# Mamba-2 scan and gated feed-forward: a 64-column scan state, multiplied with C in four 32-row products

## The chip, the cores and the metric

The kernel runs on one core of a Trainium2 chip. The time is that of one execution on the device, in microseconds (us); the kernel before took 407.95 us, the median of nine runs that lay between 407.56 and 408.33 us. The engines are called by the profile's names: PE multiplies matrices (PEld is its weight load), DVE, ACT and POOL work element by element, SP issues the DMAs.

## What is computed

Four sequences of 768 steps pass through a scan with 8 heads, of 32 channels and 16 state entries each. In the reference the scan goes in chunks; the kernel's own chunks are 128 steps long. Everything is 32-bit floating point.

```
for each chunk:
    cum   = cumsum(log a)
    M     = (C @ B^T) * exp(cum_i - cum_j) * causal
    y     = M @ x  +  (C @ state) * exp(cum)
    state = exp(sum log a) * state  +  sum_j B_j x_j exp(cum_last - cum_j)
tokens = y of the 8 heads side by side          # 3072 x 256
h      = tokens @ w_in                          # 3072 x 2048
out    = (h * cos(h)) @ w_out                   # 3072 x 256
```

The term that matters here is C @ state: for each head a 16 x 32 state is multiplied with the 16 rows of C of that head.

## The kernel before, in words

The work is cut in 6 chunks `c` of 128 steps. The four sequences `b` of a chunk make 512 tokens, and for each chunk the feed-forward goes through 16 slices `f` of 128 hidden columns. The main loop runs over n = (c, f), 96 steps and two more to finish. A step issues `first(n)` (h: two products of 128x128 weights with 512 tokens, tile hp, L373), `gate(n)` (cosine and product, DVE and ACT), and `second(n-2)` (four products with the 256 columns of w_out, tile o, L401). Between these, in the same step, one piece of the next chunk's scan is issued: `turn`, `intra` and `finish` of one sequence take three steps in turn (f = 3 to 14). So the order of PE's instructions is written out by hand, and the schedule is manual: every engine runs its own in that order.

For one sequence of a chunk, all 8 heads of 16 state entries lie in the 128 partitions, head h in rows 16h to 16h+15.

- `turn` transposes B and C (L290, L291). `bcT[:, 0]` is B, `bcT[:, 1]` is C times the decay (L299). `cT` holds two copies of C: `slot` is a column pair of ones and zeros that keeps in copy t the rows of heads whose number within its pair is t (L295).
- `intra` multiplies B and C of heads in four products (L309). Each uses 32 rows, that is one pair of heads, and writes 256 columns to a bank of its own. DVE multiplies the result with the decays (m, L313, two halves of four heads).
- `finish` makes y, transposed, in PSUM: 256 rows (8 heads of 32 channels) by 128 steps, as two blocks t of 128 rows (heads 0 to 3 and 4 to 7). First comes C @ state (L327): the state tile is 128 rows by 256 columns with zeros wherever row and column are of different heads, so that two products of 128 rows, 128 columns of weights and 128 moving columns give all heads at once. Then eight products (L331), one for each head, with 32 columns of weights, add M @ x. ACT copies y out (L336).
- At the end of `finish`, in chunks 1 to 4, `sum_up` makes B^T x in PSUM (s_ps, L348): four products, one for each pair of heads, 32 rows by 64 columns, of which the two blocks off the diagonal are of no use. `carry` (DVE) spreads s_ps over the 256 columns and masks it with `own` (L358), and adds the state before times its decay (L362). For chunk 0, `sum_up` and `carry` are issued in the loop's steps 1 and 2.

`own` is made at the start, on DVE and POOL (L218 to L221); `slot` is a sum of its columns (L225, L227). PSUM for the scan is a rotation of two pairs of banks (`pair`, tag "scan"): tp, two times g, y and s_ps take the pairs in turn, so that a tile waits until the one before the last was read.

In chunk 0 `finish` has no state term; it is given a bank by a tag, and fills with products that nobody reads (L94). From n = 0 to 13 the weights of the feed-forward, which arrive as 64-bit words, are also converted (`grade`, `join`: ACT, POOL, DVE).

Of the kernel before, what the change touches and what calls it, by code (L numbers as in the profile page):

```python
# [8 lines left out]
FP32 = mybir.dt.float32  # L9
# [3 lines left out]
ALU = mybir.AluOpType  # L13
# [12 lines left out]
def kernel(  # L26
# [23 lines left out]
    V, ACT, G, PE = nc.vector, nc.scalar, nc.gpsimd, nc.tensor  # L50

    NB, H, S, D = x.shape
    N = B.shape[-1]
    P = 128
# [5 lines left out]
    HH = H // 2  # L60
# [3 lines left out]
    HP = H // 2  # L64

    const = ctx.enter_context(tc.tile_pool(name="const", bufs=1))
    loads = ctx.enter_context(tc.tile_pool(name="loads", bufs=3))
    rows = ctx.enter_context(tc.tile_pool(name="rows", bufs=NB))
    scan = ctx.enter_context(tc.tile_pool(name="scan", bufs=2))
    states = ctx.enter_context(tc.tile_pool(name="states", bufs=NB + 1))  # L70
# [8 lines left out]
    def bank(shape, name, tag):  # L79
        return psum.tile(shape, FP32, tag=tag, bufs=2, name=name)  # L80

    def pair(name):

        return psum.tile([P, 2, 4 * P], FP32, tag="scan", bufs=2, name=name)
# [6 lines left out]
    def fill(dst, times=1):  # L91

        for _ in range(times):
            PE.matmul(dst, lhsT=ones, rhs=ones.unsqueeze(1).to_broadcast([P, dst.shape[1], P]),  # L94
                      start=True, stop=True, skip_group_check=True)
# [27 lines left out]
    def load_along(c, seqs=range(NB)):  # L123
# [15 lines left out]
        out=a_in, in_=a.rearrange("(u b) h (c p) -> (b h c) u p", u=NU, p=P))  # L139
# [65 lines left out]
    for n in (0, 2, 1, 3, 4, 5):  # L205
# [8 lines left out]
    unit = const.tile([P, HH, P], FP32, name="unit")  # L214
    V.tensor_copy(out=unit, in_=ident.unsqueeze(1).to_broadcast([P, HH, P]))

    own = const.tile([P, H, D], FP32, name="own")
    V.memset(own, 1.0)  # L218
    G.affine_select(out=own, in_=own, pattern=[[-N, H], [0, D]], compare_op=ALU.is_ge,
                    fill=0.0, base=0, channel_multiplier=1)  # L220
    G.affine_select(out=own, in_=own, pattern=[[N, H], [0, D]], compare_op=ALU.is_ge,  # L221
                    fill=0.0, base=N - 1, channel_multiplier=-1)

    slot4 = const.tile([P, HH], FP32, name="slot4")
    V.tensor_tensor(out=slot4, in0=own[:, 0:HH, 0], in1=own[:, HH:H, 0], op=ALU.add)  # L225
    slot = const.tile([P, 2], FP32, name="slot")
    V.tensor_tensor(out=slot, in0=slot4[:, 0:2], in1=slot4[:, 2:4], op=ALU.add)  # L227

# [14 lines left out]
    scaled, lam, reach, state, part, yT = {}, {}, {}, {}, {}, {}  # L243
# [73 lines left out]

    def finish(c, b, tag=None, fills=0):
        (bcT, m), xr = part.pop((c, b)), raw[c][1]
        y = (pair("y")[:, 0] if tag is None else bank([P, 4 * P], "y", tag)  # L320
             ).rearrange("p (k i) -> p k i", k=4)
        fill(y[:, 2:4], fills)
        y = y[:, 0:2]
        if c > 0:
            s = state[c - 1, b].rearrange("p h d -> p (h d)")
            for t in range(2):
                PE.matmul(y[:, t], lhsT=s[:, t * P:(t + 1) * P], rhs=bcT[:, 1],  # L327
                          start=(t == 0), stop=False, skip_group_check=True)
        for h in range(H):
            q, t = h % 4, h // 4  # L330
            PE.matmul(y[32 * q:32 * q + 32, t], lhsT=xr[:, b, h], rhs=m[:, h],  # L331
                      start=(c == 0 and t == 0), stop=True, tile_position=(0, 32 * q),
                      skip_group_check=True)
        if b == 0:
            yT[c] = two.tile([P, 2, TB], FP32, tag="yT", name="yT")
        ACT.copy(out=yT[c][:, :, b * P:(b + 1) * P], in_=y)  # L336
        if 0 < c < NC - 1:
            sum_up(c, b, pair("s_ps")[:, 0, 0:2 * D])
            carry(c, b)

    sums = {}

    def sum_up(c, b, s_ps):

        xr, sc = raw[c][1], scaled.pop((c, b))
        for q in range(4):
            two_ = slice(2 * q, 2 * q + 2)
            PE.matmul(s_ps[32 * q:32 * q + 32], lhsT=sc[:, two_].rearrange("p h n -> p (h n)"),  # L348
                      rhs=xr[:, b, two_].rearrange("p h d -> p (h d)"), start=True, stop=True,
                      tile_position=(0, 32 * q), skip_group_check=True)  # L350
        sums[c, b] = s_ps

    def carry(c, b):

        s_ps = sums.pop((c, b))
        state[c, b] = new = states.tile([P, H, D], FP32, tag="state", name="state")
        by_two = "p (k t) d -> p k (t d)"
        V.tensor_tensor(out=new.rearrange(by_two, k=HP),  # L358
                        in0=s_ps.unsqueeze(1).to_broadcast([P, HP, 2 * D]),
                        in1=own.rearrange(by_two, k=HP), op=ALU.mult)  # L360
        if c > 0:
            V.scalar_tensor_tensor(out=new, in0=state.pop((c - 1, b)),  # L362
                                   scalar=reach[c, b][:, P - 1:P], in1=new,
                                   op0=ALU.mult, op1=ALU.add)


    hp, turns, gT, o, o_full = {}, {}, {}, {}, {}
# [59 lines left out]
    decays(0, 2, 1)  # L427
    turn(0, 1)
    finish(0, 0, "o")
    intra(0, 1)  # L430
    grade(*order[0])
    spread_a(3, ("o", "h"))
    decays(0, 3, 0)
    decays(0, 3, 1)
    turn(0, 2, "h")
    finish(0, 1, "o", 1)
    intra(0, 2)
    turn(0, 3, "h")
    grade(*order[2])
    join(*order[0])  # L440
    finish(0, 2, "o", 1)
    intra(0, 3)
    grade(*order[1])
# [14 lines left out]
    for n in range(NC * NF + LAG):  # L458
        c, f = divmod(n, NF)
        rest = None  # L460
        if n < NC * NF:
            if f == 0 and c > 0:
                load(c + 2)
            first(n)
            if n == 1:
                for b in range(0, NB, 2):
                    s_ps = pair("s_ps")
                    for t in range(2):
                        sum_up(0, b + t, s_ps[:, t, 0:2 * D])
            if n + 3 < len(order):  # L470
                rest = grade(*order[n + 3], later=True)
            if n + 2 < len(order):
                join(*order[n + 2])
            for b in ((0, 1), (2, 3))[n - 1] if 0 < n < 3 else ():
                carry(0, b)
            gate(n)
            if rest:
                rest()
        if n >= LAG:
            second(n - LAG)  # L480
        if c + 1 < NC:
            b, j = divmod(f - 3, 3)
# [4 lines left out]
            b, j = divmod(f - 2, 3)  # L487
# [37 lines left out]
```

## Time and profile before

| | |
|---|---|
| median of nine runs | 407.95 us (407.56 to 408.33) |
| the profiled execution | 407.94 us, of which its span of instructions is 406.2 us |
| PE busy | 399.3 us, 2086 matmul instructions |
| DVE busy | 266.4 us, 412 instructions |
| ACT busy | 173.4 us |
| POOL busy | 43.6 us |
| granted clock of PE | 0.999 |

A 32-bit product appears in the trace as two matmul instructions and two weight loads, so L327 has 80 of them for 20 calls of `finish` with two products each. A row of a timeline gives the start, the time to the end of its last instruction, engine, line, operation, tiles and shapes, and the number of instructions that were merged. Matmuls overlap in the pipeline: their durations are longer than the time each one adds, and the distance from one start to the next is what counts. Of a wait, the profile names the engine and line that released it.

### The profile page before, as it was taken

Reading aid. Unit: us, or ns where it says so; the run is one execution under the profiler, and the core shown is the slowest. Engines: PE = TensorE matmul, PEld = TensorE weight load, DVE = VectorE, ACT = ScalarE, POOL = GpSimd, SP = SyncE. Lnnn points to the kernel's source line nnn. Section 1 sums busy time; section 2 is a strip of 40 time slices with the busy share of each in tenths; the row PEclk is TensorE's granted clock in tenths of the full one; section 3 lists DMA queues with packets and bytes.
Section 4 is the critical chain, followed back from the end, with each engine's and each line's share of the span. In section 5 each row is a group of like instructions: output and inputs, shape, how many; then the busy total and the mean of one; then the engine's idle time right before and its main releaser. Section 6 shows DMA issues by size and latency. Waiting matters only on the chain.

```text
span 406.2 us, 5538 instructions
## 1 busy us (share of the span) xinstructions
PE 399.3 (98%) x2086; PEld 261.7 (64%) x2086; DVE 266.4 (66%) x412; ACT 173.4 (43%) x329; POOL 43.6 (11%) x62
## 2 busy tenths in 40 slices
PE   8999999999999999999999999999999999999996
PEld 5646666666666666667666666666666566666664
DVE  6989999946767755677664677674576764433342
ACT  2576666434343424434334433433434343433332
POOL 2266555300000000000000000000000000000000
PEclk9999999999999999999999999999999999999999
DMA  7989899491111092110174211120100000100001
GB/s 112 270 255 223 232 261 181 124 112 53 52 52 53 13 158 64 53 51 3 52 122 61 71 34 52 53 78 1 54 0 2 0 0 2 52 0 2 0 1 52
DMA packets 106650, 30.53 MB, mean 75 GB/s; under 512 B 75328, under 2 KB 102528, under 8 KB 106624
## 3 DMA queue, kind: packets, MB, share of 16 engines
q1 hardware_dynamic: 106096, 29.92, 32.1%
q8 instruction: 16, 0.26, 0.3%
q10 hardware_dynamic: 528, 0.26, 0.2%
q14 instruction: 10, 0.08, 0.1%
HBM read 26.84 MB, written 3.34 MB: 74 GB/s over the span
## 4 chain that ended last, share of the span: by engine, by line
PE 94%; SPq 2%; DMA 1%; ACT 1%; DVE 1%; issue 0%; DVEq 0%
PE hp L373 42%; PE o L401 41%; PE g L309 4%; PE y L331 3%; PE y L327 2%; SPq L112 2%; DMA words<-in_moe_w_in_dram 1%; PE tp L290 1%; PE tp L291 1%; PE s_ps L348 0%; PE y L94 0%; ACT w L384 0%; DVE m L313 0%; DVE gT L386 0%; DVE w L379 0%
## 5 line engine op out<-in xcount | busy, mean ns | idle before, releaser
L373 PE MATMUL hp<-yT,w_in 128*128 128x512 f32 x384 | 184.8, 604 | 0.7 <-DVE gT L386 0.7
L401 PEld LDWEIGHTS o<-w_out,gT 128*128 128x128 f32 x768 | 145.9, 190 | 59.9 <-issue 44.0
L401 PE MATMUL o<-w_out,gT 128*128 128x256 f32 x768 | 181.1, 379 | 0.0
L377 ACT ACTIVATE k<-hp 128x512 int32<-128x512 f32 x96 | 57.3, 597 | 125.5 <-PE hp L373 125.4
L386 DVE TENSOR_TENSOR gT<-hp,w 128x512 f32<-128x512 f32 x96 | 66.3, 690 | 65.4 <-ACT w L384 65.4
L379 DVE SCALAR_TENSOR_TENSOR w<-hp,k 128x512 f32<-128x512 f32 x96 | 66.0, 687 | 62.4 <-ACT k L377 61.1
L373 PEld LDWEIGHTS hp<-yT,w_in 128*128 128x128 f32 x384 | 67.8, 190 | 58.4 <-issue 54.2
L384 ACT ACTIVATE w<-w,quarter 128x512 f32<-128x512 f32 x96 | 69.3, 722 | 77.8 <-DVE w L379 77.8
L274 DVE TENSOR_TENSOR_SCAN lam<-arow,unit 128x512 f32<-128x512 f32 x40 | 48.5, 1212 | 0.0
L313 DVE TENSOR_TENSOR m<-g,lam 128x512 f32<-128x512 f32 x48 | 30.7, 681 | 1.1 <-PE g L309 0.9
L283 POOL TENSOR_TENSOR sc<-bc,lam 128x128 f32<-128x128 f32 x20 | 8.2, 412 | 199.6 <-DVE lam L274 194.7
L295 ACT ACTIVATE cT<-tp,slot 128x128 f32<-128x128 f32 x48 | 14.6, 353 | 9.5 <-PE tp L291 9.5
L309 PE MATMUL g<-cT,bcT 32*128 32x256 f32 x192 | 17.2, 426 | 1.4 <-ACT bcT L297 1.4
L331 PE MATMUL y<-m,xr 128*32 128x128 f32 x384 | 15.8, 279 | 0.2 <-DVE m L313 0.2
L175 POOL TENSOR_SCALAR mag<-mag 128x512 f32<-128x512 f32 x16 | 13.0, 812 | 9.4 <-ACT mag L174 9.3
L195 DVE SCALAR_TENSOR_TENSOR mag<-words,mag 128x512 uint32<-128x512 uint32 x16 | 13.5, 841 | 0.6
L336 ACT COPY yT<-y 128x256 f32<-128x256 f32 x24 | 8.9, 372 | 11.0 <-PE y L331 11.0
L309 PEld LDWEIGHTS g<-cT,bcT 32*128 32x128 f32 x192 | 7.5, 182 | 9.0 <-issue 6.2
L327 PEld LDWEIGHTS y<-bcT,state 128*128 128x128 f32 x80 | 12.0, 191 | 1.4 <-DVE m L313 0.4
L327 PE MATMUL y<-bcT,state 128*128 128x128 f32 x80 | 12.3, 276 | 0.0
L174 ACT ACTIVATE mag<-words 128x512 f32<-128x512 f32 x16 | 10.8, 678 | 2.0 <-DMA words<-in_moe_w_in_dram 2.0
L331 PEld LDWEIGHTS y<-m,xr 128*32 128x32 f32 x384 | 8.9, 109 | 4.3 <-DVE m L313 1.4
(48 smaller groups left out, 152.1 us busy)
## 6 DMA issues: line engine op xcount, KB each, us to landing
arow<-a_cut SPq DMA_DIRECT2D x20, 512.0 KB
words<-in_moe_w_in_dram SPq DMA_DIRECT2D x8, 512.0 KB
words<-in_moe_w_out_dram SPq DMA_DIRECT2D x8, 512.0 KB
out_dram<-ob SPq DMA_DIRECT2D x10, 256.0 KB
xr<-in_x_dram SPq DMA_DIRECT2D x4, 512.0 KB
along<-a_all SPq DMA_DIRECT2D x20, 64.0 KB
xr<-in_x_dram SPq DMA_DIRECT2D x8, 128.0 KB
bc<-in_B_dram SPq DMA_DIRECT2D x4, 256.0 KB
```

The costliest lines, as they stand in the source:

```text
L274: V.tensor_tensor_scan(out=lam[c, b][:, hs].rearrange("p h i -> p (h i)"), data0=rows_.rearrange("p h i -> p (h i)"), data1=unit.rearrange ...
L295: ACT.activation(cT[:, t], tp[:, 1], AF.Copy, scale=slot[:, t:t + 1])
L309: PE.matmul(g[u // 2][:, u % 2, 0:2 * P], lhsT=bcT[r, 0], rhs=cT[r].rearrange("p t i -> p (t i)"), start=True, stop=True)
L313: V.tensor_tensor(out=m[:, hs].rearrange("p (k t) i -> p k (t i)", k=2), in0=g[u][:, :, 0:2 * P], in1=l[:, hs].rearrange("p (k t) i -> p k ...
L327: PE.matmul(y[:, t], lhsT=s[:, t * P:(t + 1) * P], rhs=bcT[:, 1], start=(t == 0), stop=False, skip_group_check=True)
L331: PE.matmul(y[32 * q:32 * q + 32, t], lhsT=xr[:, b, h], rhs=m[:, h], start=(c == 0 and t == 0), stop=True, tile_position=(0, 32 * q), skip ...
L373: PE.matmul(hp[n], lhsT=w_in[:, k, f * P:(f + 1) * P], rhs=yT[c][:, k], start=(k == 0), stop=(k == KT - 1))
L377: ACT.activation(k, hp[n], AF.Copy, bias=0.25, scale=INV_2PI)
L379: V.scalar_tensor_tensor(out=w, in0=hp[n], scalar=INV_2PI, in1=k, op0=ALU.mult, op1=ALU.subtract)
L384: ACT.activation(cos, cos, AF.Sin, bias=quarter, scale=TWO_PI)
L386: V.tensor_tensor(out=gT[n], in0=hp.pop(n), in1=cos, op=ALU.mult)
L401: PE.matmul(o[c][b], lhsT=g[:, b * P:(b + 1) * P], rhs=w_out[:, f], start=(f == 0 and (last or b % 2 == 0)), stop=(f == NF - 1), skip_grou ...
```

## The change

The state tile keeps, for each row, only the 64 columns of its own pair of heads (two blocks of 32), and the block of the other head is zero. The product with C becomes four: 32 rows (one pair of heads) by 64 columns of weights, each with a tile position of its own in PE's array. Products 0 and 1 write rows 0 to 63 and 64 to 127 of one bank, products 2 and 3 the same rows of a second bank. For chunk 0 the code keeps its one bank.

`carry` works on 64 columns: for chunk 0 one DVE instruction (s_ps times `slot`), later one DVE instruction (state times decay plus s_ps, to a new tile `whole`) and one POOL instruction that masks it with `slot`. `own` shrinks from 256 columns to 8.

```diff
-    own = const.tile([P, H, D], FP32, name="own")
+    own = const.tile([P, H], FP32, name="own")
     V.memset(own, 1.0)
-    G.affine_select(out=own, in_=own, pattern=[[-N, H], [0, D]], compare_op=ALU.is_ge,
+    G.affine_select(out=own, in_=own, pattern=[[-N, H]], compare_op=ALU.is_ge,
                     fill=0.0, base=0, channel_multiplier=1)
-    G.affine_select(out=own, in_=own, pattern=[[N, H], [0, D]], compare_op=ALU.is_ge,
+    G.affine_select(out=own, in_=own, pattern=[[N, H]], compare_op=ALU.is_ge,
                     fill=0.0, base=N - 1, channel_multiplier=-1)
...
-    V.tensor_tensor(out=slot4, in0=own[:, 0:HH, 0], in1=own[:, HH:H, 0], op=ALU.add)
+    V.tensor_tensor(out=slot4, in0=own[:, 0:HH], in1=own[:, HH:H], op=ALU.add)
...
     def finish(c, b, tag=None, fills=0):
         (bcT, m), xr = part.pop((c, b)), raw[c][1]
-        y = (pair("y")[:, 0] if tag is None else bank([P, 4 * P], "y", tag)
-             ).rearrange("p (k i) -> p k i", k=4)
-        fill(y[:, 2:4], fills)
-        y = y[:, 0:2]
         if c > 0:
-            s = state[c - 1, b].rearrange("p h d -> p (h d)")
-            for t in range(2):
-                PE.matmul(y[:, t], lhsT=s[:, t * P:(t + 1) * P], rhs=bcT[:, 1],
-                          start=(t == 0), stop=False, skip_group_check=True)
+
+            y = pair("y")[:, :, 0:P]
+            for q in range(4):
+                r, p = slice(32 * q, 32 * q + 32), 64 * (q % 2)
+                PE.matmul(y[p:p + 64, q // 2], lhsT=state[c - 1, b][r].rearrange("p t d -> p (t d)"),
+                          rhs=bcT[r, 1], start=True, stop=False, tile_position=(32 * q, p),
+                          skip_group_check=True)
+        else:
+            y = bank([P, 4, P], "y", tag)
+            fill(y[:, 2:4], fills)
+            y = y[:, 0:2]
...
     def carry(c, b):
-        s_ps = sums.pop((c, b))
-        state[c, b] = new = states.tile([P, H, D], FP32, tag="state", name="state")
-        by_two = "p (k t) d -> p k (t d)"
-        V.tensor_tensor(out=new.rearrange(by_two, k=HP),
-                        in0=s_ps.unsqueeze(1).to_broadcast([P, HP, 2 * D]),
-                        in1=own.rearrange(by_two, k=HP), op=ALU.mult)
-        if c > 0:
-            V.scalar_tensor_tensor(out=new, in0=state.pop((c - 1, b)),
-                                   scalar=reach[c, b][:, P - 1:P], in1=new,
-                                   op0=ALU.mult, op1=ALU.add)
+
+        s_ps = sums.pop((c, b)).rearrange("p (t d) -> p t d", t=2)
+        mask = slot.unsqueeze(2).to_broadcast([P, 2, D])
+        state[c, b] = new = states.tile([P, 2, D], FP32, tag="state", name="state")
+        if c == 0:
+            V.tensor_tensor(out=new, in0=s_ps, in1=mask, op=ALU.mult)
+            return
+        whole = scan.tile([P, 2, D], FP32, tag="whole", name="whole")
+        V.scalar_tensor_tensor(out=whole, in0=state.pop((c - 1, b)),
+                               scalar=reach[c, b][:, P - 1:P], in1=s_ps,
+                               op0=ALU.mult, op1=ALU.add)
+        G.tensor_tensor(out=new, in0=whole, in1=mask, op=ALU.mult)
```

## The prediction

> **What bounds the kernel now.** I read the busy times first, then the chain of work that ended last, then PE's waits, and then the timeline of PE around `finish`.
>
> ```profile
> PE 399.3 (98%) x2086; PEld 261.7 (64%) x2086; DVE 266.4 (66%) x412; ACT 173.4 (43%) x329; POOL 43.6 (11%) x62
> ...
> PE 94%; SPq 2%; DMA 1%; ACT 1%; DVE 1%; issue 0%; DVEq 0%
> PE hp L373 42%; PE o L401 41%; PE g L309 4%; PE y L331 3%; PE y L327 2%; SPq L112 2%; DMA words<-in_moe_w_in_dram 1%; PE tp L290 1%; PE tp L291 1%; PE s_ps L348 0%; PE y L94 0%; ACT w L384 0%; DVE m L313 0%; DVE gT L386 0%; DVE w L379 0%
> ```
>
> PE is busy nearly all of the span and is 94% of the chain. A busy PE could still be a PE that is held up, so its waits come next.
>
> ```profile
> PE g L309 <- ACT bcT L297: 1.4, 3, 0.9
> PE warm L94 <- DVE quarter L212: 1.1, 1, 1.1
> PE hp L373 <- DVE gT L386: 0.7, 1, 0.7
> PE y L331 <- DVE m L313: 0.2, 1, 0.2
> ```
>
> That is all, 3.4 us, and all of it before 28 us. Since matmuls are pipelined, a short hold can hide in a busy PE; the distances between starts show two more, named below, of 0.04 and 0.14 us. Otherwise what an instruction adds is the distance from its start to the next. So the time moves with what PE's queue holds, and with nothing else unless something new comes late.
>
> **The place of the change on PE.** This is one `finish` (chunk 1, sequence 1); the other 19 have the same steps to within a few ns, but for the very first.
>
> ```profile
> 55.38 0.38 PE L401 MATMUL o<-w_out,gT 128*128 128x256 f32 x1
> 55.59 0.61 PE L327 MATMUL y<-bcT,state 128*128 128x128 f32 x4
> 56.13 0.64 PE L331 MATMUL y<-m,xr 128*32 128x128 f32 x16
> 56.59 0.29 PE L348 MATMUL s_ps<-xr,sc 128*32 128x64 f32 x8
> 56.81 1.13 PE L373 MATMUL hp<-yT,w_in 128*128 128x512 f32 x2
> ```
>
> From the last o to the first y of L331 it is 0.75 us; single starts, to the ns, make it 216 + 537. The 216 is the ordinary step of an o product (256 columns). The 537 is four instructions (two products, two each) at 109 ns, and then 101 ns before L331 begins: the last L327 instruction is followed by L331 after 205 ns, not 109, because L331 takes 32 columns of the array at a time and the ones before took all of it. I call this a **switch**; L331's first weights, too, are loaded only then.
>
> What four 32-row products cost is shown by g (L309), which has four of them with 256 moving columns:
>
> ```profile
> 63.81 0.38 PE L401 MATMUL o<-w_out,gT 128*128 128x256 f32 x1
> 64.12 0.71 PE L309 MATMUL g<-cT,bcT 32*128 32x256 f32 x8
> 64.76 1.13 PE L373 MATMUL hp<-yT,w_in 128*128 128x512 f32 x2
> ...
> 64.44 0.39 PE L309 MATMUL g<-cT,bcT 32*128 32x256 f32 x4
> ```
>
> The last line is the second half of the same eight (from a later window). The eight start as two groups of four, and within a group 7 ns apart: the four products run side by side. From the last o to the first group it is 309 ns, that is 216 plus a switch of about 94; to the second group 320, that is 216 plus 104 of weight load that nothing hides; from there to hp 324, that is 216, 20 of stagger and a switch of 88.
>
> **Part 1, the product with C.** The instruction orders of the two programs differ here by just this: at each of 20 places two L327 products become four, of 64 columns of weights and 128 moving columns. If they run side by side like g's, the steps are:
> - last o to the first group: 309, as for g.
> - first to second group: 109 for 128 columns, and the exposed load. It is 104 for 128 columns of weights (g) and 25 for 32 (L331: first group to second 134 where the next ones are 109). Between these lie 64 columns; I take half of 104, 52. Together 161.
> - second group to L331: 109, stagger 20, switch 90: 219. L331's own first load is in both kernels.
>
> Sum 689 ns against 753: 64 ns less, 19 times, 1.22 us. The first `finish` is different: its L327 starts 355 after the o before, as it waits for a bank that DVE reads until 42.71 us (m), and it takes 641. There the switch costs nothing, since PE waits anyway: 355 + 161 + 219 = 735 against 996. The second half of m ends at 43.31, and L331's second four heads would come at 43.39, so up to 20 ns of the 261 go; 0.24 us. Together **1.46 us**.
>
> The bounds of this part. A switch from one partition of the array to another isn't in the trace: L331 to s_ps (both 32 columns wide) costs none, every other one 88 to 95. If it is free, 20 x 90 = 1.8 us more are gained. If both groups' loads are exposed, at 52 to 104, 20 x (52 to 104) = 1.0 to 2.1 us are given back.
>
> **Part 2, carry.** L358 (424 ns, 20 times) and L362 (485, up to 673 beside POOL, 16 times) become one DVE instruction of 64 columns from PSUM. L299, which reads 128 columns of PSUM, takes 292; a line through it and L358 gives 226 for 64. For bounds, at least 165 (the smallest DVE rows with two inputs are 168) and at most L362's 485. DVE is relieved of about 11.5 us, beside PE, which waits for DVE nowhere after chunk 0 but in two places: the first `finish` above, whose m hangs on ACT's bcT (DVE idles 0.36 us before L299 at 38.1 us) and so doesn't come sooner; and an hp at 31.1 us, where the step from o is 259 instead of 216 because the gT before it (L386) stands behind two carries. That one loses its 43 ns: **0.04 us**.
>
> **Part 3, the mask on POOL.** 16 new instructions of 64 columns; L283, 128 columns, is 412 ns, so between 206 and 412; I take 250. What is behind it in POOL's queue: in chunk 1 (four times) mag (L175) and the join of weights (L199); later only sc. Mag waits for ACT, idle 1.11 and 1.26 us before two of them, as the next step's k and Abs come first, while the mask is ready some 0.6 us after s_ps. So it is covered; without cover it would be 4 x 0.4 = 1.6 us at most, and only if weights become late, which hp shows nowhere now. The state itself is read only a chunk later: the one written at 58 us at 120. POOL also slows DVE when they run together (L362 is 483 alone and up to 673 beside POOL); in chunk 1 m is still 0.26 us ahead of L331 at the second `finish`, and later over 2 us. Nothing on the path.
>
> **Part 4, the start.** `own` shrinks: L219 and L221 (450 and 444 ns on POOL) become two of at least 104 (POOL's smallest row), and cut comes about 0.6 us sooner. The chain at the start doesn't pass there: SP issues loads until 10.74, the weights' first words land at 15.09 and ACT goes on from them. Nothing gained. If that cover weren't there, 0.6 us.
>
> Sum: 1.46 + 0.04 = 1.5 us of the profiled 407.94, which is 0.01 below the median. That gives **406.4 us** (span 404.7).
>
> **A rule that speaks against it.** Products 0 and 1 take different rows of the array and write the same bank, in different partitions. No row of this trace has that: g's four have a bank each, and L331's four share a bank but take all rows. The Trainium skill, TensorEngine Tiling (Array Packing), Gotcha 1: PSUM Pressure, says that different row tiles can't access one PSUM bank at the same time. By that rule the four would go at best two at a time, and the time would be that of the first rival. I go with the rows, as each of the two ways of sharing runs four wide by itself.
>
> **Rivals.**
> 1. *Products that share a bank take turns* (slower). For it: no row shows two row tiles in one bank. Against: L331's four column tiles share one and start 7 ns apart. Two at a time means four groups instead of two: 2 x 109 x 20 = 4.4 us on top of the forecast, 410.8. The point from which it decides is one group more: 109 - 64 = 45 ns a `finish`, 0.9 us, 408.8. With none side by side, eight groups, 6 x 109 x 20 = 13.1 us on top, 419.5.
> 2. *The switch between two tiled partitions is free* (faster). For it: L331 to s_ps. Against: that is the same partition. 406.4 - 1.8 = 404.6.
> 3. *The gain is eaten by exposed loads and switches* (no change): four narrow products side by side, but both loads exposed. For it: g's first load. Against: g's second is hidden behind 216 ns; here there are 109 to hide 52. 407.4 to 408.5.
>
> **How the numbers follow.** Forecast 0.62, with a range of its own of 405.4 to 407.1 (half a switch either way); rival 2 0.08; rival 3 0.11; rival 1 0.19, of which 410.8 is the likeliest. Leaving out rival 1 leaves 0.81, so the range runs from rival 2 to the upper end of rival 3, to just below its one extra group: 404.4 to 408.7. About 0.2%, 0.8 us, is what a measurement of this kernel tells from no change: below 407.1 are the forecast and rival 2, 0.70; within it rival 3, 0.11; above, rival 1, 0.19.
>
> **What would show it.** In the profile after: the state products as two groups of four, 7 ns apart, 0.16 us between; L331 0.38 us after their first start and 0.69 after the last o. Four groups: rival 1. A distance from the last group to L331 of 0.13 instead of 0.22: rival 2. DVE busy about 11 us lower, with PE waits unchanged. I am wrong if PE waits anew, for m, the mask or weights, or if the groups are more than two.

## The result and the profile after

The changed kernel takes 406.77 us, the median of nine runs (406.51 to 407.06); before, with more runs, it is 408.17. The ratio is 0.9964, its 95% interval 0.9955 to 0.9973: 1.5 us faster (the two medians differ by 1.40). The profiled execution took 407.06 us (span 405.3), the slowest of the nine.

The page of the changed kernel, busy times and chain:

```profile
PE 397.7 (98%) x2166; PEld 254.0 (63%) x2166; DVE 257.6 (64%) x396; ACT 173.4 (43%) x329; POOL 48.0 (12%) x78
...
PE 94%; SPq 2%; DMA 1%; ACT 1%; issue 1%; DVE 1%; DVEq 0%
PE hp L378 42%; PE o L406 41%; PE g L309 4%; PE y L334 3%; SPq L112 2%; PE y L325 2%; DMA words<-in_moe_w_in_dram 1%; PE tp L291 1%; PE tp L290 1%; PE s_ps L351 0%; PE y L94 0%; ACT w L389 0%; DVE m L313 0%; DVE w L384 0%; DVE gT L391 0%
```

PE has 80 matmul instructions more and is busy 1.6 us less. The chain has nearly the same shares.

The second `finish` of the main loop, in the changed kernel's timeline of PE (start, length, engine, line, tiles, shapes, count); the last row is from a later window, which cuts off the first half of the eight:

```profile
55.77 0.38 PE L406 MATMUL o<-w_out,gT 128*128 128x256 f32 x1
56.08 0.45 PE L325 MATMUL y<-bcT,state 32*64 32x128 f32 x8
56.45 0.64 PE L334 MATMUL y<-m,xr 128*32 128x128 f32 x16
56.91 0.29 PE L351 MATMUL s_ps<-xr,sc 128*32 128x64 f32 x8
57.14 0.70 PE L378 MATMUL hp<-yT,w_in 128*128 128x512 f32 x1
...
56.24 0.29 PE L325 MATMUL y<-bcT,state 32*64 32x128 f32 x4
```

From o to the first state product it is 0.31 us, from there to L334 0.37 or 0.38: single starts say 309 and 378 ns, 687 where there were 753. The eight instructions are two groups of four, 160 ns apart; within a group they start 7 ns apart (120.464, 120.470, 120.477, 120.484 us at the sixth `finish`). Eight instructions one after the other would take eight steps of 109 ns, the step of L327 in the kernel before. So all four products run side by side, those that share a bank too.

The distance from the first hp to the last o leaves the start out, and does not vary as the whole does: 379.69 us before, 378.16 after, and 378.16 again in a second profile of the changed kernel. That is 1.52 us. The profiled executions differ by less (0.88 us) since the first hp of the changed kernel came 0.65 us later in that one: its weights took 4.92 us to arrive where those of before took 4.35, and the chain at the start goes through them. In the second profile hp began 0.11 us later than before, and the execution took 406.51 us. I call the distance from first hp to last o **the loop** from here on.

### The profile page after: what moved, and what is told of

Its sections match the earlier page's. It is cut to its first block, busy times and chain, and to the rows that moved or that the text cites. A ratio compares the mean times of both kernels' runs of the same rounds, so it can differ in the third digit from the quotient of the medians.

```text
span 405.3 us, 5703 instructions
## 1 busy us (share of the span) xinstructions
PE 397.7 (98%) x2166; PEld 254.0 (63%) x2166; DVE 257.6 (64%) x396; ACT 173.4 (43%) x329; POOL 48.0 (12%) x78
## 4 chain that ended last, share of the span: by engine, by line
PE 94%; SPq 2%; DMA 1%; ACT 1%; issue 1%; DVE 1%; DVEq 0%
PE hp L378 42%; PE o L406 41%; PE g L309 4%; PE y L334 3%; SPq L112 2%; PE y L325 2%; DMA words<-in_moe_w_in_dram 1%; PE tp L291 1%; PE tp L290 1%; PE s_ps L351 0%; PE y L94 0%; ACT w L389 0%; DVE m L313 0%; DVE w L384 0%; DVE gT L391 0%
## 5 line engine op out<-in xcount | busy, mean ns | idle before, releaser
L334 PE MATMUL y<-m,xr 128*32 128x128 f32 x384 | 15.8, 279 | 0.2 <-DVE m L313 0.2
L369 POOL TENSOR_TENSOR state<-whole,slot 128x64 f32<-128x64 f32 x16 | 5.5, 341 | 79.4 <-DVE whole L366 79.4
L334 PEld LDWEIGHTS y<-m,xr 128*32 128x32 f32 x384 | 8.8, 109 | 5.4 <-issue 3.6
L199 POOL TENSOR_TENSOR w_out<-mag,last 128x512 uint32<-128x512 uint32 x8 | 10.2, 1274 | 8.8 <-DVE mag L195 6.8
```

## Experiments

The theory (A in the expectations) is that of the prediction: the time is the sum of the distances between PE's starts, made of streams, switches and exposed loads, and carry lies beside it. Its rivals are that DVE's relief pays a part, that the groups or loads are worth something else, and that a switch between two tiled partitions costs nothing.

**1. The four products alone.** State, carry and own stay at 256 columns; of the change only the four products are made, and y lies in two banks as there:

```diff
-            for t in range(2):
-                PE.matmul(y[:, t], lhsT=s[:, t * P:(t + 1) * P], rhs=bcT[:, 1],
+            for q in range(4):
+                r, p = slice(32 * q, 32 * q + 32), 64 * (q % 2)
+                PE.matmul(y[p:p + 64, q // 2], lhsT=s[r, 64 * q:64 * q + 64],
+                          rhs=bcT[r, 1], start=True, stop=False, tile_position=(32 * q, p),
...
```

> The four narrow products alone: state, carry and own stay as before (256 columns), and each product reads its own 32 rows and 64 columns of that state. Theory A (only the distances between PE's starts count, and carry lies beside them): from the last o to the first state product 309 ns, to L331's successor 378 more, as in the changed kernel, so a time of 406.7 to 407.0 us, ratio to before 0.9965. Rival B (part of the gain is DVE's relief of 11 us): no better than 407.3.

Measured: 406.88 us, ratio to the runs of before beside it (median 408.92) 0.9952 (0.9937 to 0.9967); the loop is 378.17 us, that of the changed kernel to 0.01 us. DVE is busy 266.0 us, as before. So the products alone give the whole gain, and the relief of DVE none of it.

**2. The carry alone.**

```diff
             for t in range(2):
-                PE.matmul(y[:, t], lhsT=s[:, t * P:(t + 1) * P], rhs=bcT[:, 1],
+                PE.matmul(y[:, t], lhsT=ones, rhs=bcT[:, 1],
...
```

The state of 64 columns and its carry are those of the change; the kernel leaves C times state out of the output.

> The 64-column carry with its mask on POOL alone: PE keeps two products of 128 rows and 128 columns, but these read a constant tile, so that C times state is left out of the output. Theory A: only the 43 ns hold of an hp at 31 us goes, so 408.0 to 408.2 us beside 408.17 before, ratio 1.000; DVE's busy time falls by 8 to 11 us all the same. Rival B: at least 0.4 us faster.

Measured: 408.89 us (408.92 before, beside it), ratio 1.0001 (0.9985 to 1.0016); the loop is 379.70 us, 0.015 more than before. The page's first row, where DVE's busy time has fallen by 7.9 us:

```profile
PE 398.7 (98%) x2086; PEld 261.5 (64%) x2086; DVE 258.5 (64%) x396; ACT 173.8 (43%) x329; POOL 48.0 (12%) x78
```

The hold of hp at 31 us did go, as expected: counted from the first hp, the products of hp there start 42 and then 145 ns sooner than before (with the hold, a load was exposed as well). But the gain isn't there any more 7 us later. Two timelines show where it went. Before:

```profile
37.81 0.26 ACT L297 COPY bcT<-tp 128x128 f32<-128x128 f32 x1
38.10 0.29 DVE L299 TENSOR_TENSOR bcT<-tp,reach 128x128 f32<-128x128 f32 x1 [0.36 <-ACT bcT L297]
38.42 0.73 PE L309 MATMUL g<-cT,bcT 32*128 32x256 f32 x8
```

and with the carry alone, where the first hp came 0.51 us later:

```profile
38.36 0.24 ACT L297 COPY bcT<-tp 128x128 f32<-128x128 f32 x1
38.63 0.29 DVE L299 TENSOR_TENSOR bcT<-tp,reach 128x128 f32<-128x128 f32 x1 [0.36 <-ACT bcT L297]
38.79 0.89 PE L309 MATMUL g<-cT,bcT 32*128 32x256 f32 x8
```

Counted from the first hp, ACT's bcT and DVE's L299 come when they came before (0.04 and 0.02 us later), and the eight g instructions last 0.16 us longer: the first pair of products starts at 38.786, the second at 38.979, since its bank is read by L299 until 38.92. The 0.15 us that PE won at 31 us it waits out here. The changed kernel does the same: it is 0.147 us ahead of before after that hp, and 0.010 us behind it after g.

**3. Products twice.**

```diff
-            for q in range(4):
+            for q in (0, 1, 2, 3) * 2:
```

> The changed kernel with the four state products issued twice, the second time overwriting the first. It prices two groups more, which is what products that take turns two at a time would have cost. Theory A: four groups instead of two, 2 x 109 ns at 20 places, 4.4 us on 406.8: 411.1 us, the block from first state product to L334 596 ns instead of 378. Rival C (a group of four is not worth 109 ns, since some of it lies beside loads and switches): under 410.0.

Measured: 411.59 us (ratio 1.0064, 1.0046 to 1.0082); the loop is 382.54 us, 4.37 more than the changed kernel's, where 4.4 was expected. In the timeline the first state product of the second `finish` starts at 56.44 us and L334 at 57.04:

```profile
56.44 0.67 PE L325 MATMUL y<-bcT,state 32*64 32x128 f32 x16
57.04 0.64 PE L334 MATMUL y<-m,xr 128*32 128x128 f32 x16
```

A group of four is worth 109 ns, all of it on the path. This is what the first rival would have cost, had products of one bank taken turns.

**4. Two products of 64 rows**, to tell the exposed load from the rest:

```diff
+            for t in range(2):
+                r = slice(64 * t, 64 * t + 64)
+                PE.matmul(y[:, t], lhsT=s[r, P * t:P * t + P],
+                          rhs=bcT[r, 1], start=True, stop=False, tile_position=(64 * t, 0),
...
```

State and carry are those of before; y lies in two banks.

> Two state products of 64 rows and 128 columns, one to each of two banks, from the state of 256 columns of before; everything else as in the changed kernel's finish. Half the instructions, the same two groups, but weights of 128 columns. Theory A (the exposed load goes by columns, 104 for 128 and 52 for 64): first group to second 213 instead of 161, then 109 + 7 + 88 = 204, so 417 ns from the first state product to L331's successor instead of 378: 20 x 39 = 0.8 us more than the changed kernel, 407.6. Rival F (the load term is a fixed cost of the first group): 161 + 204 = 365, 406.6.

Measured: 407.43 us, ratio 0.9989 (0.9976 to 1.0002), which alone wouldn't tell much. The loop does: 379.05 us, 0.88 more than the changed kernel's (0.8 was expected), and the block, from the first state product to M @ x (L335 here), is 422 ns (417 expected).

```profile
56.04 0.49 PE L326 MATMUL y<-bcT,state 64*128 64x128 f32 x4
56.46 0.64 PE L335 MATMUL y<-m,xr 128*32 128x128 f32 x16
```

Same two groups, half the instructions, twice the columns of weights: from the first group to the second 213 ns instead of 160, and in all 44 more a `finish`. The load goes by columns, and it decides two thirds of the gain: 66 ns with 64 columns, 22 with 128. These products also have 64 rows instead of 32, but g, with 32 rows and 128 columns, exposes the same 104 ns.

**5. No state products.**

> The changed kernel without its state products: C times state is left out of the output. Theory A (the whole block is on the path): from the last o to L334 309 ns instead of 687, 20 x 378 = 7.6 us less, 399.2 us; for the first sequence of chunk 1 less goes, since m comes late there (0.4 us), so 399.2 to 399.7. Rival G (part of the block lies in the shadow of DVE's m or of a wait): over 400.5.

Measured: 399.47 us (ratio 0.9786, 0.9773 to 0.98). The loop is 371.01 us, 7.15 less than the changed kernel's; 19 of the 20 places gave 377 or 378 ns each, the first `finish` nothing, since there the second four heads of M @ x (L331 in the kernel before) wait for m: 465 ns from the second group to the third instead of 109. So the block is on the path in full, but for the place where PE waits anyway.

**6. The products beside g.** They move from `finish` to the head of `intra`, into free columns of g's second pair of banks:

```diff
+        if c > 0:
+            y = ys[c, b] = g[1][:, :, 2 * P:3 * P]
+            for q in range(4):
+                r, p = slice(32 * q, 32 * q + 32), 64 * (q % 2)
+                PE.matmul(y[p:p + 64, q // 2], lhsT=state[c - 1, b][r].rearrange("p t d -> p (t d)"),
...
         for u in range(4):
...
-                      rhs=cT[r].rearrange("p t i -> p (t i)"), start=True, stop=True)
+                      rhs=cT[r].rearrange("p t i -> p (t i)"), start=(c == 0 or u < 2),
```

> The changed kernel with the four state products moved from finish to the head of intra, ahead of the g products, into columns of g's second pair of banks. The number of products is the same; what changes is that the partition of 32 rows by 64 columns now borders on that of 32 rows by 128 columns and no longer on 128 by 32. Theory A (a switch between two tiled partitions costs as much as any): 309 + 161 + 217 + 320 + 324 + 309 = 1640 ns of PE for a sequence, against 309 + 378 + 309 + 320 + 324 = 1640 now: 406.8 us, but for the first sequence of chunk 1, whose L331 has to wait for both halves of m (0.1 to 0.4 us). Rival D (the switch between these two is free and g's first load is hidden): 1428 ns, 20 x 0.21 = 4.2 us less, 402.5 us; free switch with the load exposed: 404.6.

Measured: 407.27 us, ratio 0.9962 (0.9947 to 0.9976); the loop is 378.39 us, 0.23 more than the changed kernel's, and the waits of the first sequence of chunk 1 are the cause. It waits 0.28 us more than the usual 309 ns before the state products, and 0.16 more before M @ x; the changed kernel has other waits there, 0.18 us in g (those of experiment 2) and 0.04 at the head of its first `finish`, and 0.44 - 0.22 is the difference. Otherwise nothing moved, for the switch went along:

```profile
103.60 0.45 PE L312 MATMUL g<-bcT,state 32*64 32x128 f32 x8
103.97 0.71 PE L317 MATMUL g<-cT,bcT 32*128 32x256 f32 x8
104.62 0.70 PE L382 MATMUL hp<-yT,w_in 128*128 128x512 f32 x1
```

From the state products to g 0.37 us, as from the state products to L334 in the changed kernel. A change from 32 x 64 to 32 x 128 tiles costs as much as one from 32 x 64 to 128 x 32 (198 ns from the last start to the next in both), and about as much as one from the whole array to 32 x 64 (309 ns where 216 is the stream). 32 x 64 directly before the whole array was not run.

**7. Beside g, in g's partition.** The state tile holds its 64 columns twice, so that the products are 32 x 128 like g's, each with the bank of its g product:

```diff
+            for q in range(4):
+                r = slice(32 * q, 32 * q + 32)
+                PE.matmul(g[q // 2][:, q % 2, 2 * P:3 * P],
+                          lhsT=state[c - 1, b][r].rearrange("p k t d -> p (k t d)"),
+                          rhs=bcT[r, 1], start=True, stop=False, skip_group_check=True)
...
+            for t in range(2):
+                for i in range(2):
+                    rows_ = slice(64 * i, 64 * i + 64)
+                    ACT.copy(out=yT[c][rows_, t, b * P:(b + 1) * P],
+                             in_=g[t][rows_, i, 2 * P:3 * P])
...
+            sum_up(c, b, g[0][:, 0, 3 * P:3 * P + 2 * D])
```

> The state product beside g once more, but in g's own partition: the state tile holds its 64 columns twice, so that each of the four products is 32 rows by 128 columns and writes columns 256 to 383 of the bank of its g product (half of its rows are of no use). L331 adds to those banks, ACT copies y out in four pieces of 64 rows, and s_ps goes to free columns of the first bank. Theory A (a switch is paid only where the partition changes, and a load behind 109 ns is hidden): 309 + 213 + 109 + 216 + 324 + 309 = 1480 ns of PE a sequence against 1640 in the changed kernel, 20 x 0.16 = 3.2 us less: 403.6 us, up to 404.0 with the waits for m and for C times decay in the first sequence of chunk 1 that the other early kernel had (0.28 and 0.16 us). Rival E (what is paid is not the partition but any first product that follows others on another tile, or the four ACT copies hold y's banks): no better than 406.0.

Measured: 419.24 us, ratio 1.026 (1.024 to 1.0281): 11 us slower than before. Theory A missed it; rival E named the ACT copies as one of its two readings. PE's waits of this kernel say why (line waited for: us in total, times, longest):

```profile
PE g L363 <- ACT yT L350: 10.9, 16, 2.0
```

L363 is s_ps. It writes a bank of which ACT reads y, and it stood behind ACT's four copies in the program, so PE waited for them in each of the 16 calls that have s_ps. So the copies did hold y's banks, by the order in which I had put s_ps behind them; whether the switch was gone this run left open, and the next one takes the wait away.

**8. The same, with s_ps ahead of the copies.**

```diff
         else:
+            if c < NC - 1:
+                sum_up(c, b, g[0][:, 0, 3 * P:3 * P + 2 * D])
             for t in range(2):
```

> The kernel before this one (state product in g's partition, beside g) with one step moved: sum_up is issued ahead of the four ACT copies of y, so that s_ps has no copy to wait for. Theory A: PE's waits for ACT's yT (10.9 us in that run) go, and 1480 ns instead of 1640 remain: 403.6 to 404.2 us, ratio to before 0.989 to 0.991. Rival E (the copies hold something else: ACT's k comes later, or the pair of banks of the next tp): PE waits appear at hp or tp, and the time is over 405.5.

Measured: 403.59 us (403.52 to 403.7), ratio 0.9892 (0.9877 to 0.9907), the fastest kernel of this study, 4.4 us faster than before by the ratio and 3.2 faster than the changed kernel beside it. The loop is 375.23 us, 2.93 less than the changed kernel's. Its timeline, against that of experiment 6:

```profile
102.30 0.38 PE L421 MATMUL o<-w_out,gT 128*128 128x256 f32 x1
102.61 0.50 PE L312 MATMUL g<-bcT,state 32*128 32x128 f32 x8
102.94 0.61 PE L317 MATMUL g<-cT,bcT 32*128 32x256 f32 x8
103.48 0.70 PE L393 MATMUL hp<-yT,w_in 128*128 128x512 f32 x1
```

From the state products to hp it is 0.87 us instead of 1.02: the switch between the two is gone, and g's first load is hidden behind the state products: g's two groups are 218 ns apart here and 320 in experiment 6. Against that, the state products' own load, of 128 columns now, exposes 105 ns instead of 51. What was given for it, POOL's masks of 128 columns (449 ns instead of 341) and 60 ACT copies more (ACT is busy 186.9 us), lies beside PE, whose waits are those of the changed kernel and one more of 0.2 us, for C times decay in chunk 1.

**9. The changed kernel again**, beside the one above:

> The changed kernel unaltered, beside the one above on the same chip: 406.8 us, ratio to before 0.9965; from the first hp to the last o 378.2 us in the trace, whenever the first hp comes.

Measured: 406.76 us, ratio 0.9967 (0.9954 to 0.9979), the loop 378.16.

## Why the prediction was right

The forecast was 406.4 us with a gain of 1.50; the gain is 1.52 in the loop and 1.5 by the ratio. The measured 406.77 lies 0.37 above the forecast, and 0.23 of that is the starting point: before, with more runs, is 408.17 and not the 407.94 that I subtracted from. The mechanism was the forecast one, but that the gain agrees to 0.02 us is partly luck, for the three parts below are off by 0.04, 0.03 and -0.05 us and nearly cancel.

- **The bound.** PE's chain was the bound and stayed it: what was put in (experiment 3) or taken out (5) appeared in the time one to one, but for the first `finish`.
- **Part 1, the block.** 689 ns against 753 were forecast; 687 against 753 are measured, 19 times 66 to 67: 1.26 us where 1.22 stood. The step that was a choice, half of g's load for 64 columns, held: 160 ns from group to group, so 51 of load. The first `finish` gave 0.27 us (from 996 ns to 728) where 0.24 was forecast.
- **The bounds of the switch.** The free switch of rival 2 is out by experiment 6 and by the 217 or 218 ns from the second group to L334. Rival 3, both loads exposed, is out by the same distance: stream, stagger and switch alone were forecast at 219, so it holds no second load.
- **Rival 1.** Products that share a bank start 7 ns apart, and the whole group costs one stream of 109 ns (experiment 3). The rule that row tiles can't use one PSUM bank at a time (the Trainium skill, TensorEngine Tiling (Array Packing), Gotcha 1: PSUM Pressure) does not hold here, where the two write different partitions of the bank. Two row tiles on the same partitions of one bank were not tried.
- **Part 2, carry, the one term that failed.** I gave 0.04 us for the hold of hp at 31 us. The hold went, and with it 0.15 us, since it had exposed a load as well; but the path there ran through ACT's bcT and DVE's L299 at 38 us, and g waited for them: nothing was gained, -0.01 us in the changed kernel and -0.015 in experiment 2. The sum is 1.26 + 0.27 - 0.01 = 1.52. `whole` takes 281 ns where I had 226. The rows of carry fell by 11.4 us together, as forecast, but DVE's busy time by 8.8 only. Most of the difference is the scan that makes `reach` (L265): in chunk 1 it now lies beside POOL's join of weights (L199), where three of them took 0.93 us each instead of 0.41, 2.0 us more in all. I had put it that POOL slows DVE when they run together; not all of POOL's work does, for beside the mask alone the same scan took 418 or 419 ns, as without it. None of this was on the path.
- **Part 3, the mask.** 341 ns on average (292 to 417) where I took 250; covered, as PE's waits show no weight that is late.
- **Part 4, the start.** Nothing gained, as forecast. But the start varies with the landing of the first weights: the first hp of the changed kernel came at 23.26 us in one execution and at 22.73 in another, a difference of a third of the whole gain.

## What to carry to other kernels

Where PE is the chain, count its starts: a small product costs its stream, and a change of the array's partition costs its own price, which for narrow products is nearly as large as the work (about 90 ns against 109); here one switch more, an exposed load and the stagger took back 152 of the 218 ns that four products side by side saved. So ask which neighbour has the same partition before splitting a product, and put the two together, even if half of the output is of no use. And a hold that is taken away at one place pays only if the next thing that PE waits for comes sooner as well.

## What the runs showed of the hardware

- A change between two partitions of the array cost 88 to 96 ns beyond the stream, between the whole array and tiles as well as between two kinds of tiles (32 x 64 to 128 x 32, 32 x 64 to 32 x 128; from 32 x 64 to the whole array was not run); products in the same partition, as state and g in experiment 8, followed each other without it.
- The first load after such a change is exposed and goes by the columns of weights: 25 ns for 32, 51 for 64, 104 for 128, read as what the first two groups are apart beyond the stream. The length of the stream did not hide it: after g the first two starts of hp are 533 ns apart in the kernel before, where 429 is the stream of 512 columns.
- Four tiles of 32 x 64, two to a bank, ran side by side at 7 ns from start to start, and so did 32-row tiles of one bank each and 32-column tiles of one bank in common.
